# Later tokens' queries and keys as rows in DRAM turned by DMA, and output products by halves of the heads, in a recurrent-memory attention kernel

## Chip, cores and metric

The kernel runs on one core of one Trainium2 chip. The metric is device time in microseconds (us) of one execution, lower is better. Engines are called by the profile's names: PE is TensorE's matmul and PEld its weight load, DVE is VectorE, ACT is ScalarE, POOL is GpSimd, SP is SyncE, which here only issues DMAs.

## What is computed

Two layers over x of 2048 tokens by 640, in bf16. The first is attention by segments of 32 tokens with a memory of 8 tokens. It is a recurrence: the memory rows of one segment's output are the memory input of the next. The second is a gated feed-forward block with a relu gate. Cut to what matters:

```python
def _A_ref(x, mem0, Wq, Wk, Wv, Wo, seg_len):          # H = 32 heads of 128, M = 8, seg_len = 32
    mask = (idx[:, None] < M) | (idx[:, None] >= idx[None, :])
    mem = mem0
    for s in range(n_seg):                              # 64 segments
        h = jnp.concatenate([mem, x[:, s * seg_len:(s + 1) * seg_len]], axis=1)   # 40 tokens
        q, k, v = (jnp.einsum('btd,dhe->bhte', h, W) for W in (Wq, Wk, Wv))
        scores = jnp.where(mask, jnp.einsum('bhqe,bhke->bhqk', q, k) * scale, -1e9)
        o = jnp.einsum('bhqk,bhke->bhqe', _softmax(scores), v)
        o = jnp.einsum('bhte,hed->btd', o, Wo)
        mem = o[:, :M, :]
        outs.append(o[:, M:, :])
def _B_ref(x, W_gate, W_up, W_down):
    gate = x @ W_gate
    return ((gate * (gate > 0)) * (x @ W_up)) @ W_down
h = x + _A_ref(_layernorm(x), ...)
return h + _B_ref(_layernorm(h), ...)
```

## The kernel before

**Tokens.** A segment has 40 tokens: 8 of memory, 24 "first" tokens and 8 "later" tokens of its own. The 8 memory rows and 24 first tokens fill 32 columns and go through the segment's own projections (`main_qk`, `main_v`). The 8 later tokens do not depend on the memory, so four segments' later tokens (a "quad", 32 columns) are projected together by `rest(q, part)`: six parts, Q, K and V for each of two groups of 16 heads. There are 16 quads. The first nine (EARLY) are projected at the start, while weights still arrive; the other seven are dealt out among the segments as filling work.

**Layout of a product.** The stationary operand has 32 columns, so four matmuls fill the four 32-column strips of TensorE at a time (`groups`). With `blocks`, strip j takes block j of 32 of each of 16 heads, so a result tile of 128 x 512 holds, in partition 32j + t, token t's elements 32j to 32j + 31 of 16 heads. A stream transpose on VectorE, which turns 32 x 32 blocks, then gives element by token, which is what the scores need.

**How later tokens travel.** `spread` evicts a Q or K part into a `tok` tile (ScalarE or VectorE), turns it into an `stg` tile on VectorE (L1555), for K re-orders it on GpSimd into a second `stg` tile (L1560), and writes it to the DRAM scratch `scr_qk` (L1563, issued by ScalarE for the first eight quads, by SP afterwards). V goes from PSUM to an `stg` tile and to `scr_v` (L1580). For each segment s, `load_rs(s)` on SP brings its share into one of two buffers `RS` (L1596 for Q and K, L1600 for V), issued during segment s - 1 as soon as segment s - 2 has used the buffer; GpSimd copies the Q part into `QT` (L1832). Segment 0 has a path of its own: GpSimd copies of `stg` into `RS` (L1568) and eight small DMAs issued by ScalarE for V (L1577).

**A segment in order.** Q and K of each group of 16 heads are evicted to `tok` and turned into `QT` and `KT` (L1967); V is evicted to `Vm`. Scores are added on a mask copied into PSUM (`seed`; L1846, and L1850 for later tokens), then exp on ScalarE, sums on TensorE, ln and exp for the reciprocal, and a multiply on VectorE. `pv(g)` (L1885, L1890) writes four banks, which two evictions bring into two halves of `oT`, 8 heads each. The output product of the 8 memory rows and the 24 first rows has two pieces. `wo_early` (L1918) takes the first 16 heads in four operations; its result is split into a high and a low part `half` (`hiev`, L1926). `wo(k)` (L1937) takes the last 16 heads in four operations, and `wo_add` adds the halves with a selecting product (L1954). The memory rows are then written by a predicated copy (`mem_next`, L1644), turned (L1647), and the next segment's Q and K can start (L1533). Later tokens' outputs are collected in `oTr` by GpSimd (L1903) and multiplied for eight segments at once (`rest_o`, L1618). After the last segment the feed-forward block runs over four blocks of 512 tokens.

**What sets the order.** Nothing is ordered by hand. A planner (`_Sched`) takes all operations with their dependencies, estimated durations and DMA latencies, ranks them by the length of the chain behind them plus a number from the table BIAS (by name and by name@segment), and deals them out to the five engines. Eviction copies may run on ScalarE or VectorE (`either`); the table ENGINE pins some by the same names. The two evictions of one group of `oT` share a name (`oTev0`, `oTev1`). Every engine executes its list in order and waits on semaphores. In `_Sched.op`, `r` lists what an operation reads and so waits for, `w` what it writes, `dur` and `lat` what the planner believes it takes. These are the two operations whose waits matter here:

```python
op("pe", f, r=[("oT", 0, 0), ("oT", 0, 1)] + [("Wo", 4 * jj) for jj in range(4)], x=[BA], dur=0.277, n=16, name="wo0")
some = [(k, i) for i in range(4)] if s == 0 else [(jj, k) for jj in range(4)]
```

Of the kernel before, what the change touches and what calls it, by code (L numbers as in the profile page):

```python
# [5 lines left out]
BF16 = mybir.dt.bfloat16  # L6
# [17 lines left out]
BIAS = {"sel2": -736.37, "ezero": -96.03, "ldxrs0": 311.45, "ldxrs1": 2241.73, "ldxra": 69.34, "ldxrl": 495.19,  # L24
    "ldxrx": -321.28, "ldxrn": -561.23, "ln1rT": -152.24, "l1r": -57.94, "ldxs0": 610.93, "ldxs1": -577.77,
    "ldxa": 621.69, "ldxl": 7.29, "ldxx": -108.37, "ldxn": 506.45, "ldxx0": -9.48, "ldxst": 157.44,
# [1199 lines left out]
def build_kernel(nc, A_x, A_mem0, A_Wq, A_Wk, A_Wv, A_Wo, A_seg_len, B_x, B_W_gate, B_W_up,  # L1226
# [278 lines left out]
    def again(pe, out, lhsT, rhs, tile, start, stop):  # L1505
# [4 lines left out]
                                outs=[pe.lower_ap(out)])  # L1510
        return pe.add_instruction(ins)  # L1511

    def groups(key, lhs, what, nm, share=True, blocks=False):


        if not share:
# [605 lines left out]
```

## Time and profile before

| what | value |
|---|---|
| median of 3 runs | 1039.61 us (1038.63 to 1040.48) |
| the profiled execution | 1036.79 us, span 1035.0 us |
| granted TensorE clock | 1.000 |
| Q, K, V products of segments (L1533, xT), three groups of 2560 matmuls | 168.6, 181.4 and 177.9 us busy |
| output products (L1918, L1937) | 91.4 and 85.9 us busy |
| RS loads of Q and K (L1596) | 63 issues by SP, 128 KB each, 0.38 us to issue (median), 2.3 us to land |
| transposing DMAs in the kernel (L1680) | 12 issues by SP, 1.27 us to issue (median), 2.9 us to land |
| writes of `scr_qk` | 32 issued by ScalarE, 6.6 us to land; 32 by SP, 2.1 us |
| evictions of `oT` | 132 on VectorE, 491 ns each; 124 on ScalarE, 437 ns each |
| HBM traffic | 53.08 MB read, 25.69 MB written |

How to read it: "busy" counts the time in which an engine executes. TensorE's matmuls are pipelined and their ends are modelled, so a busy PE may still stream slowly. A group's "idle before" is the time that its engine waited ahead of it, with what ended the wait. A line such as L1368 or L1369 is that of the helper `copy` (ScalarE and VectorE), which all evictions share; the names of the tiles tell them apart.

### The profile page before, as it was taken

The page shows a single profiled execution, that of the slowest core. Times are in us where ns is not written, and L with a number is a line of the kernel's source. Part 1 is how long each engine was busy: PE and PEld are TensorE (multiplying, and loading weights), DVE is VectorE, ACT ScalarE, POOL GpSimd, SP SyncE. Part 2 cuts the span into 40 slices and gives each one's busy share as a digit, 9 for nine tenths or more (in the row PEclk, how much of TensorE's full clock was granted, in tenths as well). Part 3 has the DMA queues.
Part 4 walks back from the last instruction along what each step waited for, and adds up shares of the span by engine and source line. Part 5 has one row for each costly group of instructions (what it writes and reads, how often), then busy time and mean ns, then how long its engine had stood idle before and what let it go on. Part 6 is the DMA issues. An engine that isn't in the chain of part 4 may idle for free. (4 is left out here: it accounts for less than half of the span.)

```text
span 1035.0 us, 52462 instructions
## 1 busy us (share of the span) xinstructions
PE 983.4 (95%) x24448; PEld 527.2 (51%) x23482; DVE 632.9 (61%) x1379; ACT 491.6 (47%) x1168; POOL 108.2 (10%) x262
## 2 busy tenths in 40 slices
PE   5989999999999999999999999999999899999998
PEld 2444555555555555555555565556555444344443
DVE  4865666668667766866676667657766652432323
ACT  2226555556556665555556455556655552121120
POOL 2151101001100100010011001100100010000000
DMA  9995111123112330321121122112221229411101
GB/s 328 405 309 134 40 45 39 38 52 87 46 34 62 74 68 24 92 56 35 50 81 49 34 56 83 48 31 68 73 51 26 76 88 223 109 36 41 32 20 51
DMA packets 131032, 85.19 MB, mean 82 GB/s; under 512 B 83636, under 2 KB 126972, under 8 KB 130812
## 3 DMA queue, kind: packets, MB, share of 16 engines
q1 hardware_dynamic: 125724, 77.54, 26.3%
q10 hardware_dynamic: 5088, 4.30, 1.2%
q8 instruction: 188, 3.08, 1.2%
q14 instruction: 32, 0.26, 0.1%
HBM read 53.08 MB, written 25.69 MB: 76 GB/s over the span
## 5 line engine op out<-in xcount | busy, mean ns | idle before, releaser
L1368 ACT ACTIVATE tok<-ps 128x512 bf16<-128x512 f32 x241 | 143.2, 596 | 160.1 <-PE ps L1533 141.6
L1533 PE MATMUL ps<-Wk,xT 128*32 128x512 bf16 x2560 | 181.4, 379 | 9.4 <-DVE xT L1647 9.3
L1533 PE MATMUL ps<-Wq,xT 128*32 128x512 bf16 x2560 | 168.6, 379 | 10.6 <-DVE xT L1647 10.0
L1533 PE MATMUL ps<-Wv,xT 128*32 128x512 bf16 x2560 | 177.9, 379 | 0.0
L1967 DVE STREAM_TRANSPOSE QT<-tok 128x512 bf16<-128x512 bf16 x128 | 90.8, 709 | 48.7 <-ACT tok L1368 46.3
L1967 DVE STREAM_TRANSPOSE KT<-tok 128x512 bf16<-128x512 bf16 x128 | 90.8, 709 | 42.6 <-ACT tok L1368 40.2
L1369 DVE CAST oT<-ps 128x320 bf16<-128x320 f32 x132 | 64.3, 491 | 76.3 <-PE ps L1890 73.2
L1533 PEld LDWEIGHTS ps<-Wq,xT 128*32 128x32 bf16 x2560 | 67.6, 96 | 80.8 <-DVE xT L1647 20.5
L1533 PEld LDWEIGHTS ps<-Wk,xT 128*32 128x32 bf16 x2560 | 64.7, 96 | 67.7 <-DVE xT L1647 18.3
L1709 ACT ACTIVATE g<-ps 128x512 bf16<-128x512 f32 (+1 forms) x56 | 33.4, 596 | 126.0 <-PE ps L1687 126.0
L1918 PE MATMUL ps<-Wo,oT 128*32 128x320 bf16 x2048 | 91.4, 300 | 1.5 <-DVE oT L1369 1.3
L1937 PE MATMUL ps<-Wo,oT 128*32 128x160 bf16 x4096 | 85.9, 233 | 6.8 <-DVE oT L1369 3.2
L1711 DVE TENSOR_TENSOR gT<-g,ps 128x512 bf16<-128x512 bf16 (+1 forms) x56 | 38.5, 687 | 85.2 <-PE ps L1687 77.8
L1937 PEld LDWEIGHTS ps<-Wo,oT 128*32 128x32 bf16 x4096 | 74.4, 96 | 21.8 <-DVE oT L1369 13.2
L1368 ACT ACTIVATE oT<-ps 128x320 bf16<-128x320 f32 x124 | 54.0, 437 | 65.2 <-PE ps L1890 62.7
L1533 PEld LDWEIGHTS ps<-Wv,xT 128*32 128x32 bf16 x2560 | 60.4, 96 | 37.3 <-DVE tok L1369 0.3
L1855 ACT ACTIVATE E<-ps 128x224 bf16<-128x224 f32 x128 | 45.7, 357 | 70.8 <-PE ps L1850 70.5
L1832 POOL COPY QT<-RS 128x256 bf16<-128x256 bf16 x64 | 25.6, 401 | 480.8 <-PE ps L1850 480.6
L1368 ACT ACTIVATE ps<-seed 128x384 f32<-128x384 bf16 x117 | 53.6, 487 | 39.0 <-DVE half L1926 38.8
L1687 PE MATMUL ps<-xn2T,Wg 128*128 128x512 bf16 x260 | 64.0, 379 | 0.0
L1687 PE MATMUL ps<-xn2T,Wu 128*128 128x512 bf16 x260 | 63.5, 379 | 0.0
L1369 DVE CAST tok<-ps 128x512 bf16<-128x512 f32 x79 | 52.0, 658 | 17.2 <-PE ps L1533 17.2
(91 smaller groups left out, 1413.1 us busy)
## 6 DMA issues: line engine op xcount, KB each, us to landing
RS<-scr_qk SPq DMA_DIRECT2D x63, 128.0 KB, 2.3
big<-in_A_x_dram SPq DMA_DIRECT2D x36, 160.0 KB, 2.4
Wq<-in_A_Wq_dram SPq DMA_DIRECT2D x10, 512.0 KB, 6.9
Wk<-in_A_Wk_dram SPq DMA_DIRECT2D x10, 512.0 KB, 7.7
Wv<-in_A_Wv_dram SPq DMA_DIRECT2D x10, 512.0 KB, 7.9
Wo<-in_A_Wo_dram SPq DMA_DIRECT2D x8, 640.0 KB, 11.4
scr_qk<-stg ACTq DMA_DIRECT2D x32, 128.0 KB, 6.6
scr_v<-stg SPq DMA_DIRECT2D x32, 128.0 KB, 2.6
```

Source lines behind the costliest of these rows:

```text
L1368: return e.activation(dst, src, ACTF.Copy)
L1369: return e.tensor_copy(dst, src)
L1533: o = pe.matmul(out, lhs[c], rhs, start=(c == 0), stop=(c == DC - 1), skip_group_check=True)
L1687: o = pe.matmul(bank(bk)[:, 0:TB], lhs(c), xT[:, :, c * 128:(c + 1) * 128], start=(c == 0), stop=(c == DC - 1))
L1709: op("act", lambda a, t=t, lo=lo, hi=hi, bg=bg: a.activation(g1[t.at][lo:128, :], bank(bg)[0:hi, 0:TB], ACTF.Relu), r=["B2"], x=[bg, t], d ...
L1711: op("dve", lambda v, t=t, lo=lo, j=j, bu=bu: v.tensor_tensor(gT[lo:128, j, :], g1[t.at][lo:128, :], bank(bu)[lo:128, 0:TB], ALU.mult), r= ...
L1832: op("pool", lambda e: e.tensor_copy(QT[:, :, 0:XR], RS[rb][:, 0:256].rearrange("p (h k) -> p h k", k=XR)), r=[("RSqk", rb)], w=["QTx"], d ...
L1855: op("act", lambda a: a.activation(E[:, g, :, 0:56], sco(BS[g]), ACTF.Exp, scale=SCALE), r=["table"], w=[("E", g)], x=[BS[g]], dur=0.36, n ...
L1918: o = pe.matmul(bank(BA)[p0:p0 + 32, 0:2 * SLICE], oT[:, 4 * jj + i, XR:40], cols(h, 2 * b2, 2 * b2 + 2), start=(i == 0 and jj < 2), stop= ...
L1937: o = pe.matmul(bank(BW)[32 * j:32 * j + 32, 0:SLICE], oT[:, 16 + 4 * jj + i, XR:40], cols(h, j, j + 1), start=(i == 0 and jj == 0), stop= ...
L1967: op("dve", lambda v, tb=tb, dst=dst: v.transpose(dst, tok[tb.at][:, :].rearrange("p (h r) -> p h r", r=32)), w=[("QT" if p == 0 else "KT" ...
```

## The change

Later tokens: the Q and K projections of `rest` use a new layout, `slots`: strip i takes whole heads (every fourth head of the group), so a result tile holds, in partition 32i + t, token t's 128 elements of four heads. It is evicted straight to one `stg` tile and written as rows into `scr_qk`, now 128 rows of 2048 elements per quad, row 4t + i. No stream transpose, no re-order on GpSimd and no `tok` tile is used there. `load_rs` reads the 32 rows of a segment with one transposing DMA into the same `RS` columns, in which the order of Q is now (head group, token, strip); the copy into `QT` puts that right, K needs nothing. Segment 0 uses `load_rs(0)` like every other, before the wait for the last Wo piece that the loads for segments 1 and 2 keep; its own copies and small DMAs are gone, and its V write has no wait for Wo.

Output products: the four operations of `wo_early` take two heads of each of two groups of four, so the first two need only the first half of `oT` and the last two the second half. `wo(k)` takes four heads in a row for every segment (before, for segment 0 alone), so it needs only half k // 2.

The planner's figures for transposing DMAs change from 0.5 and 3.5 us to 1.27 and 2.2. BIAS and ENGINE have other values nearly throughout (3465 entries of BIAS become 3349, ENGINE's 409 become 446). Of ENGINE, `oTev1` is pinned to ScalarE in 45 segments (2 before), `hiev` to ScalarE in 2 (39 before) and to VectorE in 22 (15 before).

```diff
-    scr_qk = nc.dram_tensor("scr_qk", [NQ, 4, 128, 512], BF16)
+    scr_qk = nc.dram_tensor("scr_qk", [NQ, 128, 4 * 512], BF16)
...
-               dur=0.5, lat=3.5, chan=("tp", 2), name="ln1rT", xfer=0.5)
+               dur=1.27, lat=2.2, chan=("tp", 2), name="ln1rT", xfer=0.5)
...
+                        if slots:
+                            rhs = W[p][:, c, :].rearrange("n (g x i e) -> n g x i e", g=2, x=4, i=4)[:, g, :, j, :]
+                            out = out.rearrange("p (x e) -> p x e", x=4)
...
         def spread(p, g, bk):
-            tb, t2 = _Slot("tok", range(NTOK)), _Slot("stg", range(nst))
-            either(lambda e, en: copy(e, en, tok[tb.at][:, :], bank(bk)[:, 0:512]), x=[bk, tb], dur=ev(512),
+            tb = _Slot("stg", range(nst))
+            k = 2 * p + g
+            either(lambda e, en: copy(e, en, stg[tb.at][:, :], bank(bk)[:, 0:512]), x=[bk, tb], dur=ev(512),
                    name=early + f"r{p}ev")
-
-            def turned(v, t2=t2):
-                dst = stg[t2.at][:, :].rearrange("p (m a k) -> p a m k", m=4, k=XR)
-                return v.transpose(dst, tok[tb.at][:, :])
-
-            op("dve", turned, x=[tb, t2], dur=0.71, name=early + f"r{p}Tev")
-            if p:
-                t1, t2 = t2, _Slot("stg", range(nst))
-                op("pool", lambda e, t1=t1, t2=t2: e.tensor_copy(
-                    stg[t2.at][:, :].rearrange("p (u k i) -> p u k i", k=XR, i=4),
-                    stg[t1.at][:, :].rearrange("p (u i k) -> p u k i", k=XR, i=4)), x=[t1, t2], dur=1.08 if early else 0.8, name=early + "ord")
             op("act" if early else "sp", lambda e: e.dma_start(
-                scr_qk[q, 2 * p + g, :, :], stg[t2.at][:, :]), w=[("scr_qk", q, p, g)], x=[t2], dur=0.4,
+                scr_qk[q].rearrange("(t i) n -> i t n", i=4)[:, :, 512 * k:512 * k + 512], stg[tb.at][:, :]),
+               w=[("scr_qk", q, p, g)], x=[tb], dur=0.4,
                lat=2.2, chan=("rqe", 12) if early else ("rq", 4), name=early + "rdma", xfer=0.35)
-            if q == 0:
-                k = 2 * p + g
-                op("pool", lambda e: e.tensor_copy(RS[0][:, 128 * k:128 * k + 128], stg[t2.at][:, 0:128]),
-                   w=[("RS0", k)], beside=[t2], dur=0.31, name="RS0")
 
         def values(g, bk):
             tb = _Slot("stg", [i for i in range(nst) if not 6 <= i < 10])
             either(lambda e, en: copy(e, en, stg[tb.at][:, :], bank(bk)[:, 0:512]), x=[bk, tb],
                    dur=ev(512), name=early + "rvev")
-            if q == 0:
-                for j in range(4):
-                    op("act", lambda e, j=j: e.dma_start(RS[0][32 * j:32 * j + 32, 512 + 128 * g:640 + 128 * g],
-                                                        stg[tb.at][32 * j:32 * j + XR, :].rearrange("p (i x) -> p i x", i=4)),
-                       w=[("RSv0", g, j)], beside=[tb], dur=0.7, lat=2.0, chan=("rv0", 8), name="ldrs", xfer=0.05, desc=2)
             op("sp", lambda e: e.dma_start(scr_v[q][:, :, 128 * g:128 * g + 128],
                                            stg[tb.at][:, :].rearrange("p (i x) -> p i x", i=4)),
-               w=[("scr_v", q, g)], r=[("Wo", 12)] if early else [], x=[tb], dur=0.55, lat=2.2,
+               w=[("scr_v", q, g)], r=[("Wo", 12)] if early and q else [], x=[tb], dur=0.55, lat=2.2,
                chan=("rve", 8) if early else ("rv", 4), name=early + "rvdma", xfer=0.6, desc=32)
 
         p, g = ((0, 0), (1, 0), (0, 1), (1, 1), (2, 0), (2, 1))[part]
         bk = B(kind)
-        groups([xkey] + list(go), lhs, [(p, g, bk)], early + f"r{p}", blocks=p < 2)
+        groups([xkey] + list(go), lhs, [(p, g, bk)], early + f"r{p}", slots=p < 2)
...
     def load_rs(s):
         q, m = divmod(s, 4)
         b = s % 2
-        op("sp", lambda e: e.dma_start(RS[b][:, 0:512].rearrange("p (k x) -> p k x", k=4),
-                                         scr_qk[q].rearrange("k p x -> p k x")[:, :, 128 * m:128 * m + 128]),
-           r=[("scr_qk", q, p, g) for p in range(2) for g in range(2)] + [("Wo", 12)] * (s < 3), w=[("RSqk", b)], dur=0.45, lat=2.2,
-           chan=("sq", 2), name="rsdma", xfer=0.5, desc=32)
+        op("sp", lambda e: e.dma_start_transpose(RS[b][:, 0:512].rearrange("p (x r) -> p x r", r=32), scr_qk[q, 32 * m:32 * m + 32]),
+           r=[("scr_qk", q, p, g) for p in range(2) for g in range(2)] + [("Wo", 12)] * (0 < s < 3), w=[("RSqk", b)], dur=1.27, lat=2.2,
+           chan=("sq", 2), name="rsdma" if s else "rs0dma", xfer=0.5, desc=32)
         op("sp", lambda e: e.dma_start(RS[b][:, 512:768],
                                          scr_v[q].rearrange("(j t) i x -> j (t i) x", t=32)[:, 4 * XR * m:4 * XR * m + 4 * XR, :]),
            r=[("scr_v", q, g) for g in range(2)], w=[("RSv", b)], dur=0.57, lat=2.2,
-           chan=("sv", 2), name="rsdma")
+           chan=("sv", 2), name="rsdma" if s else "rs0dma")
...
-    op("pool", lambda e: e.nop(), r=[("RS0", k) for k in range(4)], w=[("RSqk", 0)], dur=0.05, name="RS0")
+    load_rs(0)
...
-        op("pool", lambda e: e.tensor_copy(QT[:, :, 0:XR], RS[rb][:, 0:256].rearrange("p (h k) -> p h k", k=XR)),
+        op("pool", lambda e: e.tensor_copy(
+            QT[:, :, 0:XR].rearrange("p (y i) k -> p y i k", i=4), RS[rb][:, 0:256].rearrange("p (y k i) -> p y i k", k=XR, i=4)),
...
-            op("pe", f, r=[("Vm", g), ("E", g), ("RSv", rb)] + ([] if s else [("RSv0", g, j) for j in range(4)]), x=BP, dur=0.168, n=40, mode="r", name=f"pv{g}")
+            op("pe", f, r=[("Vm", g), ("E", g), ("RSv", rb)], x=BP, dur=0.168, n=40, mode="r", name=f"pv{g}")
...
-            for i in range(4):
-                def f(pe, i=i):
+            for e2, i0 in ((0, 0), (0, 2), (1, 0), (1, 2)):
+                def f(pe, e2=e2, i0=i0):
                     o = None
-                    for jj in range(4):
-                        h = 4 * jj + i
-                        for b2 in range(2):
-                            p0 = 64 * (jj % 2) + 32 * b2
-                            o = pe.matmul(bank(BA)[p0:p0 + 32, 0:2 * SLICE], oT[:, 4 * jj + i, XR:40],
-                                          cols(h, 2 * b2, 2 * b2 + 2), start=(i == 0 and jj < 2),
-                                          stop=(i == 3 and jj > 1), skip_group_check=True)
+                    for i in (i0, i0 + 1):
+                        for jj in (2 * e2, 2 * e2 + 1):
+                            h = 4 * jj + i
+                            for b2 in range(2):
+                                p0 = 64 * (jj % 2) + 32 * b2
+                                o = pe.matmul(bank(BA)[p0:p0 + 32, 0:2 * SLICE], oT[:, h, XR:40],
+                                              cols(h, 2 * b2, 2 * b2 + 2), start=(i == 0 and jj < 2),
+                                              stop=(i == 3 and jj > 1), skip_group_check=True)
                     return o
-                op("pe", f, r=[("oT", 0, 0), ("oT", 0, 1)] + [("Wo", 4 * jj) for jj in range(4)], x=[BA], dur=0.277, n=16,
+                op("pe", f, r=[("oT", 0, e2), ("Wo", 8 * e2), ("Wo", 8 * e2 + 4)], x=[BA], dur=0.277, n=16,
                    name="wo0")
...
-            some = [(k, i) for i in range(4)] if s == 0 else [(jj, k) for jj in range(4)]
+            some = [(k, i) for i in range(4)]
...
-            op("pe", f, r=[("oT", 1, 0), ("oT", 1, 1)] + [("Wo", 16 + 4 * jj) for jj in sorted({x for x, _ in some})], x=[BW],
+            op("pe", f, r=[("oT", 1, k // 2), ("Wo", 16 + 4 * k)], x=[BW],
                dur=0.277, n=32, name="wo1")
```

More of the change, by code (lines that the diff above doesn't have):

```diff
@@ L23 @@
 FPIECES = ((0, 384), (384, 1024), (1024, 1664))
-BIAS = {"sel2": -736.37, "ezero": -96.03, "ldxrs0": 311.45, "ldxrs1": 2241.73, "ldxra": 69.34, "ldxrl": 495.19,
-    "ldxrx": -321.28, "ldxrn": -561.23, "ln1rT": -152.24, "l1r": -57.94, "ldxs0": 610.93, "ldxs1": -577.77,
-    "ldxa": 621.69, "ldxl": 7.29, "ldxx": -108.37, "ldxn": 506.45, "ldxx0": -9.48, "ldxst": 157.44,
[626 rows of a table removed]
-ENGINE = {"ldmev": "act", "er0ev": "dve", "er0Tev": "act", "r0ev": "act", "r0Tev": "act", "r1ev": "act",
-    "Q0ev": "act", "Q0Tev": "act", "K0Tev": "act", "Q1ev": "dve", "Q1Tev": "dve", "K1Tev": "act",
-    "seed1": "act", "hiev": "act", "osbev": "dve", "osrev": "act", "l1r@0": "act", "Q0ev@1": "act",
[73 rows of a table removed]
+BIAS = {"sel2": -853.71, "ezero": -376.32, "ldxrs0": -125.57, "ldxrs1": 1909.01, "ldxra": -137.5,
+    "ldxrl": 776.69, "ldxrx": -462.75, "ldxrn": -878.93, "ln1rT": -184.51, "l1r": -379.16, "ldxs0": 642.68,
+    "ldxs1": -1132.81, "ldxa": 936.59, "ldxl": 387.06, "ldxx": 335.41, "ldxn": 415.31, "ldxx0": -308.29,
[13 rows of a table added]
+    "woadd": 116.04, "rsdma": -257.97, "memcp0": 612.64, "memcp1": -178.13, "osbev": -58.99, "odma": -1150.21,
[594 rows of a table added]
+ENGINE = {"l1r": "act", "ldmev": "dve", "er0ev": "dve", "Q0ev": "act", "Q0Tev": "act", "K0Tev": "act",
+    "Q1ev": "dve", "Q1Tev": "dve", "K1ev": "act", "K1Tev": "act", "V1ev": "dve", "seed1": "act", "hiev": "dve",
+    "oTev1": "act", "osbev": "act", "l1r@0": "act", "Q0ev@1": "act", "K0ev@1": "act", "Q1ev@1": "act",
[81 rows of a table added]
 class _Slot:
@@ L1511, in again, with groups @@
         return pe.add_instruction(ins)
-    def groups(key, lhs, what, nm, share=True, blocks=False):
+    def groups(key, lhs, what, nm, share=True, blocks=False, slots=False):
         if not share:
@@ L1669, in ln2 @@
             op("sp", lambda e: e.dma_start_transpose(xn2T[0][:, u, :].rearrange("p (c t) -> p c t", c=DC), big[at.at][:, :]),
-               r=["late"], w=[("xn2T", 0, u)], x=[at], dur=0.5, lat=3.5, chan=("tp", 2), name=nm + "T", xfer=0.5)
+               r=["late"], w=[("xn2T", 0, u)], x=[at], dur=1.27, lat=2.2, chan=("tp", 2), name=nm + "T", xfer=0.5)
             return
@@ L1680, in ffn @@
             op("sp", lambda e, u=u: e.dma_start_transpose(xT[:, u, :].rearrange("p (c t) -> p c t", c=DC), scr_n[4 * b + u]),
-               r=[("scr_n", 4 * b + u)] + (["B1", ("osb", 1)] if home else []), w=[("xn2T", home, u)], dur=0.5, lat=3.5, chan=("tp", 2), name="xnld")
+               r=[("scr_n", 4 * b + u)] + (["B1", ("osb", 1)] if home else []), w=[("xn2T", home, u)], dur=1.27, lat=2.2, chan=("tp", 2), name="xnld")
         def proj(bk, lhs, key, more=(), hold=(), writes=()):
@@ L1783, in build_kernel @@
                 sc.bias["ldm"] = 8000.0 - 20 * nload[0]
-    sc.bias["ldrs"] = 8000.0
     sc.bias["ldx"] = sc.bias["ldxr"] = 9000.0
```

1387 rows, old and new, of tables (BIAS, ENGINE) are left out of this document.

## The prediction

> **What bounds the kernel now.** I read the page's head and slices first, then the three stages by windows, then TensorE's waits in each stage, then one boundary between segments in order of time, and last the groups that the change touches.
>
> ```profile
> span 1035.0 us, 52462 instructions
> PE 983.4 (95%) x24448; PEld 527.2 (51%) x23482; DVE 632.9 (61%) x1379; ACT 491.6 (47%) x1168; POOL 108.2 (10%) x262
> ...
> PE   5989999999999999999999999999999899999998
> ```
>
> TensorE is busy 95% of the span and no other engine comes near. It is idle for 1035.0 - 983.4 = 51.6 us, and a change of order can win back only that and what hides inside "busy". The windows (time, PE, PEld, DVE, ACT and POOL busy, clock, DMA share) say where it lies:
>
> ```profile
> 0.00:90.20 90.20, 73.84 (x1420) 33.06 (x1412) 56.24 (x110) 27.29 (x60) 28.61 (x56) 1.00 0.91 319
> 90.20:837.50 747.30, 717.32 (x21616) 410.37 (x20868) 512.48 (x1159) 423.55 (x1034) 77.80 (x203) 1.00 0.21 55
> 850.00:1035.00 185.00, 180.36 (x1099) 77.47 (x898) 57.65 (x98) 34.67 (x61) 0.00 (x0) 1.00 0.29 78
> ```
>
> The start (to the first write of the memory rows, L1644, at 90.2) has 16.4 us of idle TensorE, the 63 further segments 30.0, the feed-forward part 4.6. From one L1644 to the next, the 62 intervals in the timeline add up to 746.75 us: mean 12.04, shortest 11.67, twelve at 11.72 or less, six over 12.5. The surplus over the shortest is 746.75 - 62 x 11.67 = 23.2 us. So a segment is a recurrence of about 11.7 us that other work stretches a little. Its idle TensorE, by who ends it (total, times, longest):
>
> ```profile
> PE ps L1533 <- DVE xT L1647: 19.3, 41, 0.6
> PE ps L1937 <- issue: 2.5, 6, 1.1
> PE ps L1937 <- DVE oT L1369: 2.2, 4, 0.7
> PE ps L1954 <- issue: 1.3, 2, 0.7
> PE ps L1618 <- issue: 0.9, 1, 0.9
> PE ps L1937 <- ACT oT L1368: 0.7, 1, 0.7
> PE ps L1918 <- DVE oT L1369: 0.7, 3, 0.2
> ```
>
> The largest, 19.3 us before the next Q and K (L1533), waits for memory rows written and turned on VectorE; no edit touches that step. The output products (L1918, L1937) wait 2.2 + 0.7 + 0.7 = 3.6 us for evicted oT. One boundary in order of time:
>
> ```profile
> 400.06 0.44 ACT L1368 ACTIVATE oT<-ps 128x320 bf16<-128x320 f32 x1 [1.03 <-PE ps L1890]
> 400.06 0.49 DVE L1369 CAST oT<-ps 128x320 bf16<-128x320 f32 x1 [0.67 <-PE ps L1890]
> 400.06 0.52 PEld L1618 LDWEIGHTS ps<-Wo,oTr 128*32 128x32 bf16 x16
> 400.61 1.21 PEld L1937 LDWEIGHTS ps<-Wo,oT 128*32 128x32 bf16 x64
> 402.20 0.23 DVE L1644 CAST_PREDICATED xm<-turn,ps 128x64 bf16<-128x64 uint16 x1 [0.72 <-PE ps L1511]
> ```
>
> The two halves of oT leave PSUM side by side on ScalarE and VectorE; the product of the second 16 heads starts when both are there, with an unrelated L1618 product as cover.
>
> **Output products by halves.** No matmul is added or removed (L1918 x2048, L1937 x4096 stay). The first two of four L1937 operations now need the first half alone. If the halves run side by side, the start moves from 0.49 us (VectorE's half) to 0.44 (ScalarE's): 0.05 x 62 = 3.1 us. If ScalarE takes both, the first two operations run from 0.44 to 0.44 + 1.21/2 = 1.05, and the second half is there at 2 x 0.44 = 0.88: no wait either. The table of engines pins that eviction to ScalarE in 45 segments (2 before), so this split carries it. Bounds: 0 and 3.6 us, the idle time above. I take **-3**; the row and the 0.05 agree.
>
> **Queries and keys as rows.** Removed, by group:
>
> ```profile
> L1555 DVE STREAM_TRANSPOSE stg<-tok 128x512 bf16<-128x512 bf16 x64 | 44.1, 698 | 13.2 <-DMA scr_qk<-stg 6.2 <-POOL stg L1560 3.1 <-ACT tok L1368 1.9
> L1560 POOL COPY stg<-stg 128x512 bf16<-128x512 bf16 x32 | 35.1, 1096 | 65.7 <-DVE stg L1555 62.3 <-DMA scr_qk<-stg 2.5
> L1832 POOL COPY QT<-RS 128x256 bf16<-128x256 bf16 x64 | 25.6, 401 | 480.8 <-PE ps L1850 480.6 <-POOLq L1823 0.2
> ```
>
> That is 44.1 us of VectorE and 35.1 us of GpSimd, and with the first segment's direct path four GpSimd copies (1.2 us) and eight ScalarE DMA issues of 0.68 us (5.4 us). Evictions from PSUM stay, one staging tile instead of two or three.
>
> In the start this lies on TensorE's path. The window 57 to 64 us has 5.19 us of PE in 7.00: a GpSimd reorder ends ScalarE's wait, and that ends TensorE's:
>
> ```profile
> 63.44 0.60 ACT L1368 ACTIVATE stg<-ps 128x512 bf16<-128x512 f32 x1 [2.91 <-POOL stg L1560]
> 64.09 2.13 PE L1533 MATMUL ps<-Wv,xr 128*32 128x512 bf16 x36 [1.90 <-ACT stg L1368]
> ```
>
> In the start TensorE also waits 1.7 us for VectorE's tok (it alternates evictions and turns from 31 to 41 us), 1.2 for its stg (0.6 in L1533, 0.6 in L1885), 0.9 for its oT and 0.4 more for ScalarE's stg. Together 1.9 + 0.4 + 1.7 + 1.2 + 0.9 = 6.1 us. Weights still arrive until about 49 us (DMA share over 1.0 from 12 to 57 us), so the part before that partly becomes a wait for weights. I take two thirds: **-4**, bounds -6.1 and 0. If the cover fails and the rows of segment 0 come late, the next paragraph prices it.
>
> **Segment 0's load** now goes out to DRAM and back. K rows of quad 0 exist at about 39.5 us (last Wk piece 37.1, one 1.08 us product, an eviction), the write lands in 6.6 (median of L1563 on ScalarE), the turning DMA takes up to 2.9 to issue and 9.3 to land among weight loads (longest L1680): 58 us, against scores at 57.06 now. At 58 TensorE still has V products of nine quads, 18 x 1.08 = 19 us, as cover; they now run from 59 to 90 us. The wait sits on SP, and the eight Wo loads (issued 49.7 to 62.0, landing 11.4) may queue behind it; the first use of Wo is at 85.9, so they have 12 us. Cost 0, bounds 0 and +3 if the cover is gone.
>
> **Turning DMA per segment.** SP issues 63 plain loads of 0.38 us now and turns of 1.27 (medians of L1596 and L1680): +0.9 us each, 57 in all. SP's issues add up to 3.3 us per segment in the timeline, so 4.2 of 12.0: hidden. Landing 2.9 instead of 2.3. The load goes out after a segment's second scores (409.24) and is used after the next segment's (421): 12 us of cover. Behind the longer issue stand the V rows, the memory rows' write (L2005) and the x loads; the latter two have half a segment or more. Cost 0, bounds 0 and +1.
>
> [...]
>
> **The strided copy into QT** (L1832) now picks every fourth element: priced by L1560's strided 512 elements, 1.096/2 = 0.55 us instead of 0.40. It has 8 us of cover; VectorE's oT waits behind it 12 times (2.7 us), so 12 x 0.15 = 1.8 at most. I take 0.
>
> **In the segments** 28 turns of 0.7 us leave VectorE, which is idle there a third of the time: **-1**, bounds 0 and -4. **The order** itself is re-dealt: almost every bias differs. What it can win is bounded by the surplus, -23.2; what it can lose by the spread in this trace: the best eight intervals in a row average 11.82, the worst 12.25, so a loop like its worst stretch costs 62 x (12.25 - 12.04) = +13, one like its best -14. I take 0, since neither end is nearer.
>
> **Sum:** -3 - 4 - 1 = **-8 us**, a span near 1027. The profiled execution took 1036.79 in all, 1.8 more than its span, and the median is 2.8 above that; I carry the difference over: 1039.6 - 8 = **1031.6**. A measurement of this kernel tells 0.2%, 2.1 us, from no change.
>
> **Rivals.**
> *Slower: ScalarE serves both halves late.* Place: the 45 boundaries where both oT evictions are pinned to it. Decides when ScalarE starts more than 1.05 - 0.88 = 0.17 us after the pv product, because an eviction of half (0.44) or a seed (0.49) stands ahead. A full seed ahead costs 0.49 - 0.17 = 0.32 each, 45 x 0.32 = 14.4; half of them 7.2. With -4 at the start: 1050 or 1043, I say 1047. Against: ScalarE now idles 65.2 us over 124 such evictions, ended by pv, so it is mostly free. For: it takes 45 more evictions, 20 us.
> *Slower: instructions come late.* TensorE's "issue" idle in the loop is 2.5 + 1.3 + 0.9 us, one of 1.06 inside an L1937 product at 536.3, and the queue of kind instruction moves 188 packets of 16 KB. A new order puts page ends elsewhere, and turns share the DMA engines; two more per eight segments of 1 us would be +16, less 8: 1047. For: the stretch with 128 instructions in 1.2 us. Against: only nine such waits now. [...]
> *No change.* Weights pace the start, and halves side by side leave the 19.3 us wait as the only one: 1039.6.
> *More: the order also takes half the surplus,* -11.6: 1020.
>
> **How the numbers follow.** Forecast 0.45 (its own range 1025 to 1037), more 0.14, no change 0.10, ScalarE late 0.24, instructions late 0.07. So faster 0.59, same 0.10, slower 0.31. The range 1020 to 1047 leaves out half of the more and half of the two slower cases, and nothing else: about 0.2.
>
> **What would show it.** First L1644 near 86 us and no POOL-ended wait before it; VectorE near 567 us (44 less for turns, 22 less for evictions moved to ScalarE) and GpSimd near 81; L1937's wait for oT near zero; mean interval near 11.98; RS loads as transposes landing in 3 us with QT never waiting for DMA. Wrong if L1937 waits for ScalarE's oT, if "issue" grows past 10 us, or if segments average over 12.04.

## The result

The changed kernel takes **1064.47 us** (median of 4 runs, 1062.96 to 1066.15); the kernel before 1039.12 (median of 4, 1038.61 to 1040.48). The ratio is 1.0242, with a 95% interval of 1.0223 to 1.0261: slower by 25 us, where the prediction had 8 us faster.

The head of the page of the changed kernel and, of its slices, those of TensorE, its granted clock and the DMA engines:

```profile
span 1061.2 us, 52141 instructions
...
PE 988.2 (93%) x24448; PEld 523.2 (49%) x23482; DVE 600.7 (57%) x1316; ACT 483.8 (46%) x1167; POOL 72.9 (7%) x226
...
PE   5576899999999999999999999999999989999998
...
PEclk9897999999999999999999999999999999999999
DMA  9766422121422322131123213121321228301001
```

VectorE (632.9 to 600.7 us) and GpSimd (108.2 to 72.9) have less to do. But TensorE's slices 2 to 5 (27 to 133 us) now read 5, 7, 6, 8 where they read 9, 8, 9, 9, and the granted clock reads 8 and 7 in the second and the fourth. So the loss lies in the start. Measured from one first write of the memory rows (L1618, formerly L1644) to the next:

| stage | before | after | difference |
|---|---|---|---|
| start, to the first write of the memory rows | 90.2 us | 127.8 us | +37.6 |
| 62 intervals between segments | 746.8 (mean 12.04) | 736.7 (mean 11.88) | -10.1 |
| the rest | 198.1 | 196.7 | -1.4 |

The loop did what was forecast and more; the start lost nearly four times as much. Two windows (time, PE, PEld, DVE, ACT, POOL, clock, DMA share, GB/s) show how, first of the changed kernel, then of the kernel before:

```profile
31.00:41.00 10.00, 1.87 (x20) 0.79 (x24) 0.71 (x1) 0.60 (x1) 0.00 (x0) 0.66 1.01 399
50.00:57.00 7.00, 5.75 (x104) 2.70 (x108) 1.66 (x3) 1.78 (x4) 0.00 (x0) 1.00 0.28 99
```

```profile
31.00:41.00 10.00, 8.89 (x164) 3.57 (x160) 8.97 (x15) 0.76 (x3) 0.00 (x0) 1.00 1.04 410
50.00:57.00 7.00, 7.00 (x136) 3.23 (x126) 3.88 (x7) 2.08 (x5) 6.42 (x8) 1.00 1.06 370
```

Between 31 and 41 us TensorE is busy for 1.87 us of 10 (8.89 before). From 50 us the DMA engines carry 99 GB/s at a share of 0.28 (370 GB/s at 1.06 before), although weights and rows are still to come. Rows from the timelines of SP and ScalarE in that part (start, us, engine, line; ACTq and SPq are issues of DMAs):

```profile
27.32 11.12 ACTq L1546 DMA_DIRECT2D scr_qk<-stg  x2
30.28 11.62 SPq L1741 DMA_DIRECT2D Wv<-in_A_Wv_dram  x8
38.48 0.60 ACT L1358 ACTIVATE tok<-ps 128x512 bf16<-128x512 f32 x1 [10.59 <-issue]
64.10 1.64 SPq L1571 DMA_TRANSPOSE RS<-scr_qk  x1
65.79 1.13 SPq L1741 DMA_DIRECT2D Wv<-in_A_Wv_dram  x2
```

Two issues of row writes occupy ScalarE for 11.12 us, and an eviction of `tok` comes 10.59 us late. SP stops at 41.9 us until 64.1 for segment 0's rows; the last two Wv loads and all of Wo are queued behind. And once attention starts, ScalarE's short functions of segment 0 stand one by one behind an issue each:

```profile
65.42 14.40 ACTq L1546 DMA_DIRECT2D scr_qk<-stg  x6
79.87 0.36 ACT L1829 ACTIVATE E<-ps 128x224 bf16<-128x224 f32 x1 [13.88 <-DVE stg L1359]
80.72 5.66 ACTq L1546 DMA_DIRECT2D scr_qk<-stg  x1
86.42 0.34 ACT L1844 ACTIVATE rS<-lnS 128x160 bf16<-128x160 f32 x1 [5.42 <-issue]
86.45 2.90 ACTq L1546 DMA_DIRECT2D scr_qk<-stg  x1
89.40 0.49 ACT L1358 ACTIVATE ps<-seed 128x384 f32<-128x384 bf16 x1 [2.64 <-issue]
```

The 13.88 us are put down to VectorE's `stg`, but the line above shows what filled them: six issues, 14.40 us. What that does to TensorE, by who ends its waits:

```profile
PE ps L1526 <- ACT tok L1358: 9.6, 1, 9.6
PE ps L1834 <- ACT E L1829: 7.3, 2, 6.1
PE ps L1526 <- ACT stg L1358: 6.4, 6, 2.7
PE ps L1820 <- ACT ps L1358: 5.0, 1, 5.0
```

These four are 28.3 us; of them, only the wait for `stg` stood in the trace of before, with 2.3 us. In the start TensorE is idle for 127.8 - 83.3 = 44.5 us, against 16.4: +28.1. The remaining 9.5 of the 37.6 are "busy" time (83.3 against 73.8) for nearly the same matmuls (1442 and 1420) at a lower granted clock, 0.89 in the mean of the start. The kernel with whole rows, shown next, needs 75.7 us for 1441 matmuls of the same order at a clock of 1.00, so about 7.6 us go with the clock (an estimate, 83.3 - 75.7).

### The profile page after: what moved, and what is told of

Its sections match the earlier page's. It is cut to its first block, busy times and chain, and to the rows that moved or that the text cites. A ratio compares the mean times of both kernels' runs of the same rounds, so it can differ in the third digit from the quotient of the medians.

```text
span 1061.2 us, 52141 instructions
## 1 busy us (share of the span) xinstructions
PE 988.2 (93%) x24448; PEld 523.2 (49%) x23482; DVE 600.7 (57%) x1316; ACT 483.8 (46%) x1167; POOL 72.9 (7%) x226
## 4 chain that ended last, share of the span: by engine, by line
PE 84%; DMA 7%; DVE 4%; issue 1%; ACT 1%; ACTq 1%; SPq 1%; POOL 0%; DVEq 0%
PE ps L1526 43%; PE ps L1661 11%; PE ps L1912 7%; PE ps L1893 7%; DMA scr_qk<-stg 5%; PE ps L1713 4%; PE ps L1592 3%; PE ps L1859 2%; PE ps L1501 2%; PE ps L1834 2%; DMA big<-in_A_x_dram 1%; DVE xT L1621 1%; PE ps L1820 1%; DVE xm L1618 1%; ACTq L1546 1%
## 5 line engine op out<-in xcount | busy, mean ns | idle before, releaser
L1526 PE MATMUL ps<-Wq,xT 128*32 128x512 bf16 x2560 | 172.4, 380 | 18.5 <-DVE xT L1621 15.7
L1526 PE MATMUL ps<-Wk,xT 128*32 128x512 bf16 x2560 | 180.6, 379 | 0.5 <-DVE xT L1621 0.5
L1526 PE MATMUL ps<-Wv,xT 128*32 128x512 bf16 x2560 | 178.5, 380 | 0.0
L1358 ACT ACTIVATE tok<-ps 128x512 bf16<-128x512 f32 x189 | 112.9, 597 | 137.3 <-PE ps L1526 110.4
L1358 ACT ACTIVATE oT<-ps 128x320 bf16<-128x320 f32 x192 | 77.0, 436 | 78.1 <-PE ps L1864 76.0
L1526 PEld LDWEIGHTS ps<-Wq,xT 128*32 128x32 bf16 x2560 | 63.8, 96 | 91.0 <-DVE xT L1621 35.2
L1526 PEld LDWEIGHTS ps<-Wk,xT 128*32 128x32 bf16 x2560 | 64.9, 96 | 58.5 <-ACT stg L1358 3.1
L1912 PE MATMUL ps<-Wo,oT 128*32 128x160 bf16 x4096 | 84.3, 233 | 4.1 <-ACT oT L1358 3.6
L1912 PEld LDWEIGHTS ps<-Wo,oT 128*32 128x32 bf16 x4096 | 74.0, 97 | 18.4 <-ACT oT L1358 15.6
L1526 PEld LDWEIGHTS ps<-Wv,xT 128*32 128x32 bf16 x2560 | 59.9, 96 | 37.3 <-issue 0.3
L1893 PEld LDWEIGHTS ps<-Wo,oT 128*32 128x32 bf16 x2048 | 48.9, 97 | 27.3 <-ACT oT L1358 10.5
L1526 PE MATMUL ps<-Wk,xr 128*32 128x512 bf16 x640 | 47.4, 397 | 13.2 <-ACT tok L1358 9.6
L1358 ACT ACTIVATE ps<-seed 128x384 f32<-128x384 bf16 x95 | 44.6, 492 | 31.8 <-DVE half L1901 28.8
```

The lines of the kernel that those rows point to most:

```text
L1358: return e.activation(dst, src, ACTF.Copy)
L1526: o = pe.matmul(out, lhs[c], rhs, start=(c == 0), stop=(c == DC - 1), skip_group_check=True)
L1893: o = pe.matmul(bank(BA)[p0:p0 + 32, 0:2 * SLICE], oT[:, h, XR:40], cols(h, 2 * b2, 2 * b2 + 2), start=(i == 0 and jj < 2), stop=(i == 3 a ...
L1912: o = pe.matmul(bank(BW)[32 * j:32 * j + 32, 0:SLICE], oT[:, 16 + 4 * jj + i, XR:40], cols(h, j, j + 1), start=(i == 0 and jj == 0), stop= ...
```

## The experiments

**The theory.** The new write gives `scr_qk` as an access pattern whose slowest dimension is 4 (the strips); before, it was 128 rows. My conjecture, for the runs to test: if the slowest dimension sets how many of the 16 DMA engines carry a transfer, the 32 early writes (32 x 128 KB = 4.2 MB) run on four of them. At the 99 GB/s of the window above they take 42 us, at the 399 before it 10.5 (estimates). The rivals: segment 0's detour and SP's wait in front of Wo cost the time, or ScalarE's issues do.

**Write alone out.** The changed kernel with the write in whole rows:

```diff
- scr_qk[q].rearrange("(t i) n -> i t n", i=4)[:, :, 512 * k:512 * k + 512]
+ scr_qk[q][:, 512 * k:512 * k + 512]
```

> The changed kernel, with each Q or K part written to the scratch as 128 whole rows in the order of the partitions (slowest dimension 128) and not as 4 strips of 32 rows (slowest dimension 4). Bytes, packets and the planner's figures stay; the rows of the later tokens come back in another order, so that part of the result is changed. Theory A (the slowest dimension of 4 leaves the write to 4 of the 16 DMA engines, so it lands late and holds ScalarE): the first memory write (L1618) comes at 85 to 92 us instead of 127.8, the issue on ScalarE falls from 0.92 us (median) to about 0.33, and the time to 1024 to 1030 us. Theory B (the new order itself is bad in the start): first memory write still after 115 us, time above 1055 us.

1026.74 us, ratio 0.9848 (0.9821 to 0.9876). The start is 90.93 us, the loop 736.8: only the start changed. (Its later tokens come back mixed up, so it prices the write and is no replacement.) The same two windows of this kernel, and its issues (min/median/max ns, first and last start):

```profile
31.00:41.00 10.00, 8.23 (x140) 3.17 (x136) 3.73 (x6) 2.22 (x4) 0.00 (x0) 1.00 1.04 409
50.00:57.00 7.00, 6.37 (x120) 2.98 (x120) 2.42 (x5) 0.60 (x1) 0.41 (x1) 1.00 0.85 209
...
L1546 ACTq DMA_DIRECT2D scr_qk<-stg x32: 338/353/1377, 15.4 to 63.1; - x32
```

and of the changed kernel:

```profile
L1546 ACTq DMA_DIRECT2D scr_qk<-stg x32: 554/922/5682, 15.4 to 95.3; - x32
```

The median issue falls from 0.92 to 0.35 us and the longest from 5.7 to 1.4. SP still waits 8.1 us for the rows of quad 0 in this kernel (22.2 before the edit), and TensorE's waits in its start name no load of weights.

**The same write put into the kernel before**, where nothing else is changed, with 4, 16 and 8 as its slowest dimension:

```diff
- scr_qk[q, 2 * p + g, :, :]
+ scr_qk[q, 2 * p + g].rearrange("(t i) n -> i t n", i=4)
```

> The kernel before, with only the destination of its scratch write turned into 4 strips of 32 rows (slowest dimension 4, same 128 KB block, same packets); the rows of the later tokens come back in another order. Theory A: the suspected cost alone makes the start of the old kernel long too: first memory write 15 to 40 us after 90.2, time 1054 to 1080 us. Theory B: 1039 us, as before. Theory C (only SP's wait for the first segment's load ahead of the last weights costs): 1039 us, since that wait isn't in this kernel.

> The kernel before, with the destination of its scratch write turned into 16 strips of 8 rows (slowest dimension 16) in place of the 4 strips of 32 rows of e2; bytes, packets and the three-level pattern are as there, the rows of the later tokens come back in another order. Theory A (the slowest dimension sets how many DMA engines carry the write): 16 engines again, first memory write near 91 us, time 1038 to 1046 us, no stretch with the DMA share near a quarter. Rival (a three-level pattern or scattered rows as such are slow, whatever the slowest dimension): 1060 to 1080 us, as e2.

> The kernel before, with its scratch write turned into 8 strips of 16 rows, between e7 (16) and e2 (4); the rows of the later tokens come back in another order. Theory A in numbers: the busiest DMA engine carries 1/16 of 21 MB of weights and 1/k of 4.2 MB of rows, at 25 MB per ms each (99 GB/s over four engines in e2 and in the changed kernel): 63 us for k = 16, 73 for 8, 94 for 4. So the first memory write lies about 10 us behind e7's 94.5, at 100 to 108, and the time at 1050 to 1062 us. Rival (only 16 engines or not matters, or the engines aren't the reason): as e7 or as e2.

One run each, on chips where the kernel before took 1042.8 and 1042.9 us:

| slowest dimension | time | start | loop | ScalarE's issue, median and longest |
|---|---|---|---|---|
| 128 (before) | 1042.8 | 90.2 (in the trace of before) | 746.8 | 0.33, 0.83 us |
| 16 | 1047.4 | 94.5 | 752.2 | 0.53, 1.71 |
| 8 | 1056.7 | 106.9 | 749.3 | 0.59, 0.66 |
| 4 | 1074.7 | 123.5 | 751.1 | 1.00, 5.32 |

Start, loop and issues of the first row are from the trace of the kernel before, an execution of 1036.8 us; beside the experiments it took 6 us more, and no trace was taken of it there. The nearest one, with the groups of the output products alone (below), has a start of 91.5 us and a loop of 751.5. So loops of 749 to 752 us say nothing here, while the starts do: the write alone, without the rest of the change, costs 32 to 33 us. Fewer strips, longer start, step by step, and the steps of 12.4 and 16.6 us are larger than the 6.8 us between the fastest and the slowest of 13 runs of the kernel before. The working in the last expectation has 8 and 4 strips 10 and 31 us behind 16; measured are 12.4 and 29.0. The same window of the kernels with 4, with 8 and with 16 (columns as above):

```profile
71.00:78.00 7.00, 1.87 (x20) 0.51 (x20) 1.77 (x3) 0.76 (x2) 0.29 (x1) 0.75 0.27 98
```

```profile
71.00:78.00 7.00, 2.19 (x40) 0.66 (x29) 2.31 (x4) 0.60 (x1) 0.78 (x2) 0.95 0.54 191
```

```profile
71.00:78.00 7.00, 6.13 (x116) 2.83 (x112) 4.70 (x9) 1.16 (x4) 1.08 (x1) 1.00 0.48 120
```

With 4 the plateau of the changed kernel is there again, a share of 0.27 and 98 GB/s; with 8 it is 0.54 and 191, twice as much. Both are plateaus: taken microsecond by microsecond, the share is 0.27 or 0.28 with 4 strips and 0.54 or 0.55 with 8, while with 16 the mean of 0.48 is made of values from 0.06 to 0.83. Late landings cost twice over: `stg` buffers come free later (VectorE's turns wait for the writes for 6.2 us in the trace of before, 11.9 with 8 and 23.6 with 4), and with 4 ScalarE's issues swell too; with 8 they don't, their longest is 0.66. So in the kernel before with few strips, TensorE's largest added wait is for VectorE, which evicts into `tok` and turns from it. With 4 strips, then with 8:

```profile
PE ps L1533 <- DVE tok L1369: 15.8, 8, 4.0
```

```profile
PE ps L1533 <- DVE tok L1369: 8.8, 8, 3.3
```

In the trace of before this wait was 1.7 us.

**SP's wait put behind Wo.** In the changed kernel, the load of segment 0 waits for Wo like the next two:

```diff
- + [("Wo", 12)] * (0 < s < 3)
+ + [("Wo", 12)] * (s < 3)
```

> The changed kernel, with the first segment's transposing load bound to wait for the last Wo piece, as the loads for segments 1 and 2 do, so that SP issues all weights first. The write by 4 strips stays. Theory C (SP's wait ahead of the last weights is the whole loss): DMA stays busy to about 62 us, time 1024 to 1032 us. Theory A: weights arrive early, but ScalarE is still held by its issues and the rows still land late: time 1038 to 1058 us. Theory B: above 1055 us.

1069.53 us in its one run: no gain. The start does get shorter, 122.2 us for 127.8, but the first interval of the loop takes 20.5 us and the whole loop 748.6 for 736.7. The weights come earlier, but ScalarE's issues stay (median 1.28 us, longest 5.65), TensorE waits 16.0 us for ScalarE's `tok` and 10.2 for its `stg`, and the shortage of DMA has only moved:

```profile
90.00:102.00 12.00, 8.66 (x128) 3.40 (x120) 4.74 (x10) 1.58 (x4) 0.00 (x0) 0.86 0.28 98
```

As the whole loss, that rival falls; what SP's wait may have cost in the start is those 5.6 us.

**What the loop's gain is made of.** The grouping of the output products put into the kernel before (the loops of `wo_early`, `some` and the `r=` of `wo`); the same taken back from the changed kernel with whole rows; and that kernel with the old tables BIAS and ENGINE:

> The kernel before with the output products by halves alone (the two operations' loops and waits of the changed kernel, all else and both tables as before). Prediction's step: 3 us less, 1036 us, the loop's mean interval 12.00 instead of 12.04. Rival (the halves are evicted side by side, so nothing is won without the new table): 1039 us. Other rival (an order that was made for other waits is disturbed): 1041 to 1046 us.

> e1 (changed kernel with whole rows) with the output products' loops and waits of the kernel before, tables as in the changed kernel. It prices the halves under the new table, where ScalarE alone evicts the second group in 45 segments. Theory (the split carries that table): each of those boundaries waits for the second half, 0.88 instead of 0.44 us, up to 45 x 0.4 = 18 us: 1037 to 1045 us, loop's mean interval 12.05 to 12.2. Rival (the halves are worth only what they were under the old table, 2 to 3 us): 1028 to 1031 us.

> e1 with the kernel before's tables BIAS and ENGINE. It separates the edits from the new order. If the edits alone shorten the loop: 1026 to 1031 us. If the order does it: 1033 to 1042 us, and the loop's mean interval stays near 12.0.

| kernel | tables | rows | groups | ratio to before (95%) | loop |
|---|---|---|---|---|---|
| before | old | no | no | 1 | 746.8 (execution of 1036.8 us) |
| groups into before | old | no | yes | 0.9976 (0.9958 to 0.9994) | 751.5 |
| both edits, whole rows | old | yes | yes | 1.0015 (0.9993 to 1.0038) | 749.5 |
| whole rows, no groups | new | yes | no | 1.0278 (1.0257 to 1.0299) | 770.8 |
| whole rows | new | yes | yes | 0.9848 (0.9821 to 0.9876) | 736.8 |

Both edits with the old tables win nothing measurable, and their loop is 12.7 us longer than with the new ones (749.5 against 736.8). The new tables without the groups lose 34 us of loop and 12 behind it. The gain needs both. The waits of TensorE in the loop, first without the groups, then with them (both with the new tables and whole rows):

```profile
PE ps L1526 <- DVE xT L1621: 29.3, 48, 0.8
PE ps L1911 <- ACT oT L1358: 8.1, 9, 1.0
PE ps L1859 <- DVE Vm L1359: 6.1, 7, 1.5
```

```profile
PE ps L1526 <- DVE xT L1621: 15.7, 36, 0.6
PE ps L1912 <- ACT oT L1358: 3.1, 6, 0.6
```

The wait for `oT` itself is 8.1 against 3.1. The larger share shows as waits later in the segment, for the memory rows (`xT`) above all. That these grew because `oT` came late is argued and not shown: without the groups the planner also deals all work out anew.

**Keeping the rows without the slow write.** First, one DMA for each strip, so that each has 32 rows as its slowest dimension:

```diff
+ for i in range(4):
+     scr_qk[q].rearrange("(t i) n -> i t n", i=4)[i, :, 512 * k:512 * k + 512], stg[tb.at][32 * i:32 * i + 32, :]
```

> The changed kernel, with each Q or K part written by four DMAs, one per strip of 32 rows (slowest dimension 32), to the rows that the changed kernel uses; nothing is left out. Theory A: all 16 engines carry each, the start is short again; 96 more issues of about 0.35 us on ScalarE in the start (34 us of its time, which has room) cost 0 to 8 us there: 1024 to 1036 us, first memory write 88 to 98 us. Rival (ScalarE's issues are the bound, not the engines that carry the bytes): four times the issues make the start as long as in the changed kernel, 1055 us or more.

1064.43 us, ratio 1.0185 (1.0151 to 1.0219), start 108.3. The start won 19.5 us and not the 37 hoped for: ScalarE now issues 128 DMAs instead of 32, and its timeline shows

```profile
54.76 20.26 ACTq L1547 DMA_DIRECT2D scr_qk<-stg  x37
```

20 us of nothing but issues; between 13 and 90 us it evicts nothing, since from 16 us on one issue follows the other. VectorE evicts alone, and TensorE waits 16.0 us for its `stg`. So the rival holds in part: the start stays longer than with whole rows, but not as long as in the changed kernel. (Its loop is longer too, 759.9 us.)

Second, the rows in another order in DRAM: 16 strips of 8 rows in the write, and the turning DMA reads every fourth row.

```diff
- scr_qk[q].rearrange("(t i) n -> i t n", i=4)[:, :, 512 * k:512 * k + 512]
+ scr_qk[q].rearrange("(k s) n -> s k n", s=16)[:, :, 512 * k:512 * k + 512]
...
- scr_qk[q, 32 * m:32 * m + 32]
+ scr_qk[q].rearrange("(r m) n -> m r n", m=4)[m]
```

> The changed kernel, with the scratch rows renumbered: the write goes out as 16 strips of 8 rows (slowest dimension 16), and a segment's transposing load takes every fourth row, which gives it the same 32 rows in the same order as in the changed kernel. Nothing is left out. Theory A: first memory write 91 to 96 us, loop as in e1 (736.8 us), 1027 to 1034 us; the issue on ScalarE near 0.53 us, as in e7, may cost a few us in the start. Rival (rows read at a stride of 16 KB make the turning DMA late): QT waits for DMA in many segments, loop above 750 us, time above 1042 us.

**1030.84 us, ratio 0.9892 (0.9864 to 0.9921)**: nothing of the computation is left out, and it is about 1% faster than the kernel before (the changed kernel has 1.0242). Start 91.7, loop 739.4. Its slices and issues:

```profile
PE   5998999999999999999999999999999899999998
...
PEclk9999999999999999999999999999999999999999
```

```profile
L1546 ACTq DMA_DIRECT2D scr_qk<-stg x32: 546/598/1332, 15.3 to 64.6; - x32
```

Telling the planner that an issue of this write takes 0.55 us and not 0.4 was the last run:

> e9, with the planner told 0.55 us for that issue instead of 0.4, so that it deals the work out anew. If the planner's wrong figure for the issue costs in e9's start: first memory write 1 to 4 us earlier than in e9, and the same loop: 1026 to 1031 us. Rival (the tables fit one order only, and any other figure disturbs it, as in e5 and e6): 1032 us or more, with a longer loop.

1031.59 us, ratio 0.9900 (0.9874 to 0.9926): the same.

## Why the prediction was wrong

**The step that failed** is in "Segment 0's load": "the write lands in 6.6 (median of L1563 on ScalarE)", and with it "Cost 0, bounds 0 and +3". I took the duration of the old write for the new one because engine, queue and size (32 issues of 128 KB) are the same, and looked only at the read side, at the turning DMA. But the destination pattern had changed from 128 rows to 4 strips, and the write is the larger item: 4.2 MB in the very stretch in which 21 MB of weights arrive. Its price was +32 to +33 us in the kernel before (4 strips against 128) and +37 here (start 127.8 against 90.9 with whole rows).

The runs agree with the conjecture in the rate: with 4 strips a plateau of 98 and 99 GB/s at shares of 0.27 and 0.28, about a quarter of the 399 GB/s at 1.01 in the trace of the changed kernel; with 8 strips 191 GB/s at 0.54, about half; and starts of 94.5, 106.9 and 123.5 us with 16, 8 and 4. No view numbers the engines, so that four of the 16 carry the write, as the expectations have it, was not shown. At the measured 99 GB/s the 4.2 MB take 42 us (an estimate) instead of 10.5 at 399: a rival on the slower side that was not there.

**Its second half** was half seen: "The wait sits on SP, and the eight Wo loads ... may queue behind it ..., so they have 12 us". SP's wait is 22.2 us, and the last two Wv loads stand in it too. Yet the run with that wait moved won 5.6 us of start and lost more behind it, and in the whole-rows kernel 8.1 us of it stay with no wait of TensorE for weights, so it is not what decides. What decides is the slow write. In the changed kernel it reaches TensorE through ScalarE, which I had only relieved ("eight ScalarE DMA issues of 0.68 us"): its issues last up to 5.7 us, and evictions and exponentials stand behind them. In the kernel before with 4 strips it reaches TensorE mostly through VectorE's `tok`. Why an issue swells with 4 strips and not with 8 no run shows.

**"-4" in the start** did not appear even with whole rows: 90.93 against 90.16. The turns and re-orders are gone, but of the waits of 6.1 us that I had listed 3.6 are still there (3.3 for `stg` evictions, 0.3 for oT), and 1.0 for a transposing load of `xr` is new. Idle time fell only from 16.4 to 15.2 us, and busy time rose by 1.9 with 21 more matmuls ahead of the first memory rows. Weights, named for the lower bound, end no wait of TensorE there.

**"-3" for the halves**: right in size under the old tables (-0.24%, 2.5 us, interval 0.06% to 0.42%), but that is luck as far as the traces tell, for the wait that it was to remove is still there. TensorE's waits for oT in the loop, both products together, were 3.6 us before; they are 3.9 with the groups alone under the old tables and 5.7 in the changed kernel. L1912, formerly L1937, for which I had named "near zero", has 3.1 of them against 2.9 before:

```profile
PE ps L1912 <- ACT oT L1358: 3.1, 6, 0.6
PE ps L1893 <- DVE oT L1359: 2.6, 3, 1.2
```

So the sign "Wrong if L1937 waits for ScalarE's oT" came in a small way (0.7 us before), while the rival behind it, ScalarE serving both halves late for 7 to 14 us, did not. Under the new tables, taking the groups out costs 34 us of loop. I had named the 45 pinned evictions as the reason why the split matters, and 45 x 0.44 us, a ScalarE eviction more each, would be 20; where the rest comes from stays open.

**"-1" in the segments** did not show under the old tables: both edits stand at 1.0015 and the groups alone at 0.9976, so the rows rather cost there.

**"0" for the order**: the loop of the changed kernel is 10.1 us shorter than in the trace of before, and 24 longer with the new tables but without the groups. TensorE's idle time in the loop fell from 30.0 to 24.6 us: its "issue" waits from 5.2 to 0.2, the wait for memory rows, which no edit was said to touch, from 19.3 to 15.7. (The worst eight intervals in a row average 12.32 and not 12.25, so the bound on the slower side was +17.) The mean interval is 11.88; 11.98 was named, and 11.79 would have been "half the surplus". So the loop by itself landed between the forecast and the rival "more".

**Held as said:** the turning DMA per segment lands in 2.8 us (median) and is hidden (the copy into `QT` waits for it twice, both in the start); instructions do not come late (TensorE's largest "issue" wait ahead of L1912 is 0.2 us, once; in the trace of before each of the ten in the loop, 5.2 us together, ends 1.4 to 1.6 us after a 16 KB packet of kind instruction did, which is what the trace has of the rival of late instructions); GpSimd is at 73 us, 81 were named. VectorE is at 601 and not at 567: it gave 68 evictions of `oT` to ScalarE, as read from the table, and took others in exchange, as ScalarE's total (484 us, 492 before) shows. The strided copy into `QT` takes 0.41 us, not 0.55:

```profile
L1805 POOL COPY QT<-RS 128x256 bf16<-128x256 bf16 x64 | 26.4, 412 | 597.8 <-PE ps L1824 501.7
```

## What to carry to other kernels

When an edit rewrites an access pattern, the row of the old DMA is no longer its price, even with the same bytes, engine and queue: write down the slowest dimension of both sides first. Here 4 strips had a plateau at a share of 0.28 and 99 GB/s, 8 one at 0.54 and 191, and 16 none; a small one is to be priced at such a share until a run has measured it. Look then at what the issuing engine does besides: here slow writes stretched its issues from 0.35 to 0.92 us, and evictions and exponentials stood behind them. Tables that order the work belong to the edits they came with; tried apart, each looked like a loss or like next to nothing here.

## What the runs showed of the hardware

An issue became dearer with the strips alone, without any shortage: 0.33 us (128 rows) against 0.53 (16 strips, median, minimum 0.525) on ScalarE, and 0.33 against 0.55 on SP, whose writes mostly fall into the loop.

The granted clock was low around the gaps: 0.66 between 31 and 41 us in the changed kernel, where TensorE was busy for 1.87 of 10 us, 0.55 between 78 and 84, and 1.00 in both stretches with whole rows. In the kernel before with 8 strips it was 0.95 between 71 and 78 us, where TensorE was busy for 2.19 of 7, and 0.50 in the six after that. The Wk matmuls of later tokens (L1526, `xr`) average 410 ns in the start of the changed kernel, 380 in that of the kernel before (L1533). So the long waits were paid twice here: 28.1 us as idleness and about 7.6 (the estimate above) as slower matmuls.

In the list of DMA issues, the writes with 4 strips have no time to landing, in the changed kernel as in those with 4 and 8 strips in the kernel before; with 16 it is there. The lines of the changed kernel, then of the one with 16 strips:

```profile
scr_qk<-stg ACTq DMA_DIRECT2D x32, 128.0 KB
```

```profile
scr_qk<-stg ACTq DMA_DIRECT2D x32, 128.0 KB, 7.2
```

In the kernel before, the loads of V rows (`RS<-scr_v`) and the memory rows' writes (`scr_o<-osb`) have the blank too, and their patterns in DRAM also begin with 4; no run here changed those. A blank in that column is worth a look at the pattern.
